# Eight edits to the order of work in a fused recurrence and mixture-of-experts kernel on one core

## The chip, the cores and the metric

The kernel runs on one core of a Trainium2 chip, in one launch. The metric is device time in microseconds (us), the median of repeated executions. A core has TensorE (PE, matmuls and their weight loads, PEld), VectorE (DVE), ScalarE (ACT), GpSimd (POOL) and SyncE (SP), each of which takes its instructions in its own program order, and DMA queues that the engines issue to. Loads go out on SP's queue, some on POOL's and ACT's.

## The reference

```python
# 1. recurrence, B=4, H=8, S=768, D=40 (fp32)
for t in range(S):
    y[:, :, t] = einsum('bhd,bhde->bhe', r_t, state)
    Sa = einsum('bhde,bhe->bhd', state, a_t)
    state = state * w_t[:, :, None, :] - einsum('bhd,bhe->bhde', Sa, b_t) + einsum('bhd,bhe->bhde', v_t, k_t)
x = y.transpose(0, 2, 1, 3).reshape(3072, 320)
# 2. first MoE: 320 -> 1536 -> 320
x = ((x @ w_a) * (x @ w_b)) @ w_out
# 3. second MoE: 8 experts, the best one for each token
logits = x @ w_gate;  expert_idx = argmax(logits);  g = softmax(logits)[expert_idx]
out = g * (maximum(x @ w1[expert_idx], 0) @ w2[expert_idx])     # 320 -> 1024 -> 320
```

## The kernel before

The 768 steps of the recurrence are done in 12 chunks of 64. Each matmul on fp32 data is made of three or more matmuls on split values: a high part, and the rest that the high part leaves.

`phase1` walks through 13 rounds `c` of 24 slots `i`. In round `c` it runs the main stages of chunk `c` for the four batches in two pairs, prepares chunk `c+1` (the inverse of a 64x64 triangular matrix: DVE steps `tmp`, `xt`, lines 716 and 722, between transposes `t`, line 755, and matmuls `ta`, line 759), `c+2` and `c+3` (loads, range checks, cumulative decays), and lays the matmuls of MoE 1's up-projection (`pm`, line 1115, two groups of eight in each odd slot) between them. Slots of the tables `STEADY`, `LAST` (round 12) and `FIRST` (round 0) say when a piece is issued. The order on PE, DVE, ACT and POOL is the order in which the code issues it; `dv.later(n, f)` and `ot.later(n, f)` put a piece off by `n` slots. SP's order is left to a scheduler that follows the data.

What the change touches:

- **xf.** `stage5` transposes a pair's result into `pz` (PSUM, pool psA of five buffers). DVE multiplies it by the decays into `xf` (line 957) `dxf` slots later. Three slots after stage5, ACT copies `xf` to `xh` (line 1093) and POOL makes `xl` (line 1094), the inputs of `pm`. The next stage0 transposes `sgp_u` (line 666) into the buffer that `pz` gives back, and so waits for `xf`.
- **Range checks.** `spans` (line 557) is four ACT instructions `junk<-w` for each chunk, which wait for the load of `w` (line 534, SP, slot 7). ACT also copies `pm` out as `ua` (line 1118).
- **Output weights' conversion.** `wout` is a list of steps, 60 of them, on 15 pieces: a load `rawo` of 256 KB (line 1060, SP), DVE `c_f` (line 429) and ACT `c_k` (line 431), and more on DVE and ACT. `T["wout"][i]` says how many are taken in slot `i`: seven in a round, from chunk 2 on, in slots 1, 2, 6, 17, 19, 20, 22 and 23. The finished weights (`wo`, DRAM) are read by `load_w` (line 1160, POOL's queue).
- **Gates (round 12).** `gate_steps` makes eight more columns of the output weights: DVE adds the two parts to `gf` (line 1204), PE transposes it (`gt`, line 1217), ACT copies (`gft`, line 1219), PE multiplies by the gate's weights (`pg`, line 1233), ACT copies (`gs`, 1236), PE transposes (`pg`, 1225), and ACT `wh` and DVE `wl` (lines 1239 and 1240) write the columns, which the first products `py` (line 1268) read.
- **MoE 1, down.** `load` brings a tile `hf` of the hidden layer, 512 KB (line 1247, SP, three buffers); `conv` makes `hh` on ACT and `hl` on DVE (lines 1257, 1258), and then calls `load(i + 3)`. Each tile feeds 24 products `py`, and three tiles make a unit of 256 tokens. After a unit DVE chooses the expert and computes the token's place (lines 1281 to 1316), and POOL scatters the rows (line 1321).
- **MoE 2's first weights.** Towards the end of MoE 1 `first` issues the loads `r1` (lines 1452 to 1454) and `r2` (line 1460) of expert 0's weights and gathers the first rows (`x_head`, line 1515); ACT and POOL split them (lines 1469 to 1475, 1483, 1484).

Of the kernel before, what the change touches and what calls it, by code (L numbers as in the profile page):

```python
# [31 lines left out]
FIRSTX = [5, 7, 3, 8, 10]  # L32
# [7 lines left out]
def kernel_body(tc, I, out, stage="full", dbg=None):  # L40
    nc = tc.nc
    ctx = ExitStack()
    with ctx:
# [36 lines left out]
        with ExitStack() as moe:  # L80
            with tc.manual_schedule(engines={E.PE, E.DVE, E.Activation, E.Pool}):
                down = None if stage == "up" else MoeDown(tc, I, moe, psA, psM, ident, hT, wo, xs)
                phase1(tc, I, cst, drm, psA, psM, ident, hT, mk_ident, wo, xs, span, tiny, down)
                if stage == "up":
                    return
                experts = Experts(tc, I, moe, psA, psM, ident, xs, out)
                down.run(experts, span, tiny, flag)
# [45 lines left out]
def phase1(tc, I, cst, drm, psA, psM, ident, hT, mk_ident, wo, xs, span, tiny, down):  # L133
# [7 lines left out]
    def run(fs):  # L141
        for f in fs:
            f()

    conv = M.weight_steps()
    wout = M.wout_steps(wo)
# [68 lines left out]
    for c in range(NCH + 1):  # L215
        T = dict(STEADY)
# [9 lines left out]
        for i in range(24):  # L226
            run(ot.take())
            if c == NCH and down:
                if i == LAST["free"]:
                    mid.close()  # L230
                    down.begin()
                    M.spare = down.p2
                if i >= LAST["gate"]:
                    run(down.gate_steps(1))
                for j in range(3):
                    if i == LAST["load"][j]:
                        down.load(j)
                for j in range(2):
                    if i == LAST["w"][j]:
                        down.load_w(4 * j + 4)  # L240
                    if i == LAST["conv"][j]:
                        down.conv(j)
# [16 lines left out]
            if c < NCH and i == T["uload"][1]:  # L259
                A.uload(c, 1)  # L260
            if c == NCH - 1 and i == LAST["open"] and down:
                att.close()
# [79 lines left out]
            more = []  # L342
            if c < 2:
                more = conv.take(T["conv"][i] if c == 0 else FIRST["conv1"][i])
            elif c < NCH:
                more = wout.take(T["wout"][i])
            if 2 <= c < 10 and i == T["fill"] - 2:
                A.zero([zt])
            if 2 <= c < 10 and i == T["fill"]:
# [34 lines left out]
    "r0": [19, 21, 23], "r1": [7, 14, 15], "load_r": [10, 1], "score": [7, 8, 15, 19], "row": [11, 21], "relayout": 5,  # L384
    "load_w": 7, "span": [10, 11, 13, 15], "scan": [16, 17, 20, 20, 22], "inverse": 22, "vload": [9, 20], "uload": [19, 7],

    "t21a": [22, 26], "t21b": [24, 28],
    "tinv": [0, 0, 2, 3, 5, 5, 2, 2, 5, 5, 5, 5, 5, 5, 5, 5, 3, 0, 0, 0, 0, 0, 0, 0],
    "group": 2, "fill": 5, "dsg": 2, "dxf": 1, "dtake": 3, "dh": 1, "dst": 3,
}  # L390
LAST = {"open": 21, "free": 6, "w": [1, 17], "load": [14, 16, 19], "gate": 18, "conv": [21, 22]}

FIRST = {
    "order": [
# [740 lines left out]
class MoeDown:  # L1135
# [126 lines left out]
    def product(self, py, i, j, cols):  # L1262

        first, G = i * self.G % self.K, self.G
        s = slice(128 * j, 128 * j + 128)
        for k in range(G):
            for n, (l, r) in enumerate(((1, 1), (0, 0), (1, 0))):
                self.nc.tensor.matmul(  # L1268
                    py, self.pair[i][l][:, k, s], self.W[r][:, first + k, cols],
                    start=(first + k == 0 and n == 0), stop=(first + k == self.K - 1 and n == 2))  # L1270
# [149 lines left out]
class Experts:  # L1420
# [64 lines left out]

    def first(self, i):

        ops = [(i + 2, lambda: self.load1(0)), (i + 2, lambda: self.load2(0)), (i + FIRSTX[0], lambda: self.head(0)),
               (i + FIRSTX[1], lambda: self.head(1)), (i + FIRSTX[4], lambda: self.head(2))]
        ops += [(i + FIRSTX[2] + k, lambda k=k: self.split1(0, k)) for k in range(3)]  # L1490
        ops += [(i + FIRSTX[3] + k, lambda k=k: self.split2(0, k)) for k in range(4)]
        return ops
# [407 lines left out]
```

## Time and profile before

| | |
|---|---|
| median of 3 runs | 1096.92 us (1094.73 to 1098.28) |
| profiled execution | 1096.91 us, of which the span is 1095.2 us and 1.7 us lie around it |
| busy | PE 88%, PEld 84%, DVE 65%, ACT 52%, POOL 36% |
| mean granted TensorE clock | 0.938 of full speed |

One slice of the page's table is 27.4 us. The granted clock of a stretch is given as a share of 2.4 GHz, so 0.50 is 1.2 GHz. In a row of the timeline the brackets hold the engine's idle time before the instruction, and what ended it.

### The profile page before, as it was taken

The page shows a single profiled execution, that of the slowest core. Times are in us where ns is not written, and L with a number is a line of the kernel's source. Part 1 is how long each engine was busy: PE and PEld are TensorE (multiplying, and loading weights), DVE is VectorE, ACT ScalarE, POOL GpSimd, SP SyncE. Part 2 cuts the span into 40 slices and gives each one's busy share as a digit, 9 for nine tenths or more (in the row PEclk, how much of TensorE's full clock was granted, in tenths as well). Part 3 has the DMA queues.
Part 4 walks back from the last instruction along what each step waited for, and adds up shares of the span by engine and source line. Part 5 has one row for each costly group of instructions (what it writes and reads, how often), then busy time and mean ns, then how long its engine had stood idle before and what let it go on. Part 6 is the DMA issues. An engine that isn't in the chain of part 4 may idle for free.

```text
span 1095.2 us, 28147 instructions
## 1 busy us (share of the span) xinstructions
PE 968.2 (88%) x10879; PEld 915.2 (84%) x10879; DVE 713.9 (65%) x1891; ACT 572.7 (52%) x1365; POOL 397.4 (36%) x433
## 2 busy tenths in 40 slices
PE   4045478899999999999999999999998899999994
PEld 4045477799999998999999999899998899999994
DVE  8799689698989878898986832346566642222230
ACT  5357767566666666656665453333334254444540
POOL 4336444324233232324232112002215377666641
PEclk9656579899999999999999999999999999999998
DMA  8563453658696867769584234635566364444500
GB/s 206 154 163 92 101 139 99 162 120 195 139 196 153 189 169 145 183 132 199 133 181 122 64 83 134 204 114 170 179 195 190 112 215 129 147 149 143 159 16 17
DMA packets 218667, 158.59 MB, mean 145 GB/s; under 512 B 125269, under 2 KB 200630, under 8 KB 218524
## 3 DMA queue, kind: packets, MB, share of 16 engines
q1 hardware_dynamic: 205196, 137.33, 49.4%
q0 software_dynamic: 9808, 15.76, 4.7%
q10 hardware_dynamic: 3520, 3.61, 1.2%
q8 instruction: 88, 1.44, 0.6%
q14 instruction: 55, 0.45, 0.2%
HBM read 108.08 MB, written 44.60 MB: 139 GB/s over the span
## 4 chain that ended last, share of the span: by engine, by line
PE 62%; DVE 13%; DMA 8%; issue 6%; ACT 4%; POOL 4%; SPq 1%; POOLq 0%; DVEq 0%; ACTq 0%
PE pm L1115 21%; PE py L1268 10%; PE u L1562 6%; PE dn L1582 5%; PE s1p L631 3%; DVE tmp L716 3%; PE p L907 3%; DVE xt L722 3%; PE pp L891 2%; DMA out<-y,ids 2%; PE py L936 2%; PE px L836 2%; POOL l L1484 1%; PE ta L759 1%; DMA hf<-hT 1%
## 5 line engine op out<-in xcount | busy, mean ns | idle before, releaser
L716 DVE TENSOR_TENSOR tmp<-m,xt 128x126 f32<-128x126 f32 (+22 forms) x372 | 117.2, 315 | 33.1 <-DMA m<-nd 24.7
L1565 DVE SCALAR_TENSOR_TENSOR hl<-u,hh 128x384 fp32r<-128x384 f32 (+5 forms) x72 | 41.5, 580 | 139.7 <-ACT hh L1564 139.7
L1115 PE MATMUL pm<-xl,wh 128*128 128x256 f32 x576 | 130.8, 309 | 1.8 <-ACT ua L1118 1.2
L722 DVE TENSOR_TENSOR xt<-xt,tmp 128x126 f32<-128x126 f32 (+22 forms) x372 | 113.4, 305 | 9.1
L1115 PE MATMUL pm<-xh,wl 128*128 128x256 f32 x576 | 117.5, 286 | 0.0
L1115 PE MATMUL pm<-xh,wh 128*128 128x256 f32 x576 | 116.8, 285 | 0.0
L1127 DVE TENSOR_TENSOR uh<-pm,ua 128x256 f32<-128x256 f32 x144 | 59.6, 415 | 61.5 <-PE pm L1115 42.7
L1115 PEld LDWEIGHTS pm<-xl,wh 128*128 128x128 f32 x576 | 89.3, 193 | 7.6 <-ACT ua L1118 2.1
L1268 PE MATMUL py<-wh,hl 128*128 128x328 f32 x288 | 91.6, 318 | 3.3 <-DVE hl L1258 3.3
L1268 PE MATMUL py<-wl,hh 128*128 128x328 f32 x288 | 92.4, 321 | 0.6 <-DVE wl L1240 0.6
L1268 PE MATMUL py<-wh,hh 128*128 128x328 f32 x288 | 91.6, 318 | 0.0
L1115 PEld LDWEIGHTS pm<-xh,wh 128*128 128x128 f32 x576 | 91.2, 194 | 0.0
L1115 PEld LDWEIGHTS pm<-xh,wl 128*128 128x128 f32 x576 | 91.0, 194 | 0.0
L1115 PE MATMUL pm<-xl,w 128*128 128x256 f32 x288 | 82.5, 286 | 0.0
L1115 PE MATMUL pm<-xh,w 128*128 128x256 f32 x288 | 82.4, 286 | 0.0
L919 POOL TENSOR_SCALAR_AFFINE_SELECT s<-s 64x512 f32<-64x512 f32 x56 | 43.7, 781 | 102.1 <-ACT s L917 99.6
L759 PE MATMUL ta<-t,s 32*32 32x32 f32 x768 | 23.1, 200 | 59.9 <-DVE t L755 56.2
L1321 POOL DMA_INDIRECT xs<-xr,si x24 | 28.3, 1181 | 131.2 <-DVE acc L1316 77.4
L1118 ACT COPY ua<-pm 128x256 f32<-128x256 f32 x144 | 53.6, 372 | 42.6 <-PE pm L1115 39.5
L641 POOL TENSOR_SCALAR_AFFINE_SELECT s<-s 64x512 f32<-64x512 f32 x48 | 33.7, 702 | 115.3 <-ACT s L639 109.5
L1582 PE MATMUL dn<-l,hh 128*128 128x320 f32 (+3 forms) x240 | 75.0, 312 | 0.0
L1582 PE MATMUL dn<-h,hl 128*128 128x320 f32 (+3 forms) x240 | 74.0, 309 | 0.0
(276 smaller groups left out, 2810.7 us busy)
## 6 DMA issues: line engine op xcount, KB each, us to landing
hT<-uh SPq DMA_DIRECT2D x72, 256.0 KB
hf<-hT SPq DMA_DIRECT2D x36, 512.0 KB
r<-in_moe_w SPq DMA_DIRECT2D x8, 1280.0 KB
r<-in_moe_w SPq DMA_DIRECT2D x8, 1024.0 KB
bk<-in_bk SPq DMA_DIRECT2D x22, 360.0 KB
xs<-zt SPq DMA_DIRECT2D x8, 805.0 KB
m<-nd SPq DMA_DIRECT2D x44, 128.0 KB
at<-in_a SPq DMA_DIRECT2D x24, 180.0 KB
```

The source lines that it names most:

```text
L641: nc.gpsimd.affine_select(out=v, in_=v, pattern=[[0, 8], [1, C]], base=0, channel_multiplier=-1, compare_op=ALU.is_gt, fill=0.0)
L716: nc.vector.tensor_tensor(box[0], m[2 * s // R][:, s % (R // 2):s % (R // 2) + 1, s + 1:].to_broadcast([128, rows, n]), xt[:, :rows, s:s + ...
L722: nc.vector.tensor_tensor(xt[:, :rows, s + 1:], xt[:, :rows, s + 1:], box[0], op=ALU.subtract)
L759: nc.tensor.matmul(pa[b % 2][urow(b, R), R * h:R * h + R], s1[b % 2][urow(b, 0), h, R:C], t11[urow(b, 0), h, :], start=True, stop=True)
L919: nc.gpsimd.affine_select(out=s2t[q * C:q * C + C], in_=s2t[q * C:q * C + C], pattern=[[0, 8], [1, C]], base=0, channel_multiplier=-1, com ...
L1115: nc.tensor.matmul(p, l, r, start=(i == 0), stop=(i == len(seq) - 1))
L1118: nc.scalar.copy(a, p)
L1127: nc.vector.tensor_tensor(h[:, f % 2], p, a, op=ALU.mult)
L1268: self.nc.tensor.matmul(py, self.pair[i][l][:, k, s], self.W[r][:, first + k, cols], start=(first + k == 0 and n == 0), stop=(first + k == ...
L1562: nc.tensor.matmul(p, l, r, start=(i == 0), stop=(i == len(seq) - 1))
L1565: nc.vector.scalar_tensor_tensor(out=hl, in0=p, scalar=0.0, in1=hh.bitcast(F32), op0=ALU.max, op1=ALU.subtract)
L1582: nc.tensor.matmul(p, l[:, q], r[:, f], start=(f == 0 and i == 0), stop=(f == len(hs) - 1 and i == 2))
```

## The change

Eight numbers are changed: xf is computed in the slot of its transposes instead of the next; the first of the four range checks goes from slot 10 to 11; chunk 2 takes no step of the output weights' conversion before slot 5, so its first is in slot 6; in round 12 the second load of output weights is called in slot 11 instead of 17, the three first tiles `hf` in 18, 20 and 22 instead of 14, 16 and 19, and the gates start in slot 14 instead of 18; and `r2` is called three products later.

```diff
             elif c < NCH:
-                more = wout.take(T["wout"][i])
+                more = wout.take(T["wout"][i] if c > 2 or i > 4 else 0)
...
-    "load_w": 7, "span": [10, 11, 13, 15], "scan": [16, 17, 20, 20, 22], "inverse": 22, "vload": [9, 20], "uload": [19, 7],
+    "load_w": 7, "span": [11, 12, 13, 15], "scan": [16, 17, 20, 20, 22], "inverse": 22, "vload": [9, 20], "uload": [19, 7],
...
-    "group": 2, "fill": 5, "dsg": 2, "dxf": 1, "dtake": 3, "dh": 1, "dst": 3,
+    "group": 2, "fill": 5, "dsg": 2, "dxf": 0, "dtake": 3, "dh": 1, "dst": 3,
 }
-LAST = {"open": 21, "free": 6, "w": [1, 17], "load": [14, 16, 19], "gate": 18, "conv": [21, 22]}
+LAST = {"open": 21, "free": 6, "w": [1, 11], "load": [18, 20, 22], "gate": 14, "conv": [21, 22]}
...
-        ops = [(i + 2, lambda: self.load1(0)), (i + 2, lambda: self.load2(0)), (i + FIRSTX[0], lambda: self.head(0)),
+        ops = [(i + 2, lambda: self.load1(0)), (i + 5, lambda: self.load2(0)), (i + FIRSTX[0], lambda: self.head(0)),
```

DVE at the start of chunk 2, before (`c_f` is the conversion's first instruction, `t` the transposes for chunk 3's inverse, `bk` the scaling of chunk 4):

```order
L621 TENSOR_TENSOR bk4_0_2121<-bk4_0_2121,suf4_2183 120x6x64
L429 TENSOR_SCALAR c_f_2524<-rawo0_2449 128x256
L755 STREAM_TRANSPOSE t11_2_1_2576<-s1_2_1_1273 32x256 x2
L621 TENSOR_TENSOR bk4_0_2121<-bk4_0_2121,suf4_2183 120x6x64
L716 TENSOR_TENSOR tmp3_0_2601<-m3_2420,xt3_2421 128x31
```

The same place now:

```order
L621 TENSOR_TENSOR bk4_0_2121<-bk4_0_2121,suf4_2183 120x6x64
L755 STREAM_TRANSPOSE t11_2_1_2568<-s1_2_1_1273 32x256 x2
L716 TENSOR_TENSOR tmp3_0_2592<-m3_2422,xt3_2423 128x31
L621 TENSOR_TENSOR bk4_0_2121<-bk4_0_2121,suf4_2183 120x6x64
L722 TENSOR_TENSOR xt3_2423<-xt3_2423,tmp3_0_2592 128x31
```

The instruction `c_f` now comes 28 rows later, behind the first nine steps of chunk 3's inverse.

DVE in round 12, before, from `gf3` on (`uh` is the output of an up-projection, `hl` the low part of a tile `hf`):

```order
L1204 TENSOR_TENSOR gf3_11399<-wh_11026,wl_11027 128x640
L1258 TENSOR_TENSOR hl0_11436<-hf0_11280,hh0_11435 128x1024
L1204 TENSOR_TENSOR gf4_11461<-wh_11026,wl_11027 128x640
L1258 TENSOR_TENSOR hl1_11484<-hf1_11304,hh1_11483 128x1024
L1127 TENSOR_TENSOR uh11_8_11376<-pm11_9_1_11452,ua11_9_11450 128x256
L1204 TENSOR_TENSOR gf5_11490<-wh_11026,wl_11027 128x640
L1127 TENSOR_TENSOR uh11_10_11546<-pm11_10_1_11537,ua11_10_11535 128x256
L1127 TENSOR_TENSOR uh11_10_11546<-pm11_11_1_11560,ua11_11_11556 128x256
L1240 TENSOR_TENSOR wl_11027<-pg_11481,wh_11026 128x12x8
```

The same engine now, from `gf3` on:

```order
L1204 TENSOR_TENSOR gf3_11349<-wh_11026,wl_11027 128x640
L1204 TENSOR_TENSOR gf4_11405<-wh_11026,wl_11027 128x640
L1127 TENSOR_TENSOR uh11_6_11326<-pm11_7_1_11396,ua11_7_11394 128x256
L1204 TENSOR_TENSOR gf5_11430<-wh_11026,wl_11027 128x640
L1127 TENSOR_TENSOR uh11_8_11486<-pm11_8_1_11477,ua11_8_11475 128x256
L1258 TENSOR_TENSOR hl0_11526<-hf0_11427,hh0_11525 128x1024
L1240 TENSOR_TENSOR wl_11027<-pg_11425,wh_11026 128x12x8
L1258 TENSOR_TENSOR hl1_11557<-hf1_11506,hh1_11556 128x1024
L1127 TENSOR_TENSOR uh11_8_11486<-pm11_9_1_11542,ua11_9_11540 128x256
```

All of `gf` now stands ahead of `hl0`, and `wl` ahead of the last three `uh`.

SP's loads towards the end of MoE 1, before (`hf32` to `hf35` are the last tiles):

```order
L1454 DMA r1_0_12822<-in_moe2_w1 64x1024
L1460 ISA
L1460 DMA r2_0_12826<-in_moe2_w2 128x8x320
L1247 DMA hf32_12882<-hT_67 128x4x256
L1247 DMA hf33_12937<-hT_67 128x4x256
L1247 DMA hf34_12969<-hT_67 128x4x256
L1515 ISA
L1515 DMA x_head_12971<-xs_72 128x2x322
L1247 DMA hf35_13032<-hT_67 128x4x256
```

And now:

```order
L1454 DMA r1_0_12822<-in_moe2_w1 64x1024
L1247 DMA hf32_12880<-hT_67 128x4x256
L1247 DMA hf33_12935<-hT_67 128x4x256
L1460 ISA
L1460 DMA r2_0_12969<-in_moe2_w2 128x8x320
L1247 DMA hf34_12967<-hT_67 128x4x256
L1515 ISA
L1515 DMA x_head_12971<-xs_72 128x2x322
L1247 DMA hf35_13032<-hT_67 128x4x256
```

The load `r2` changes places with `hf32` and `hf33`.

## Rows read from the trace of the kernel before

**Rows 1.** The page: busy us; slices in tenths; one group (busy, mean ns | idle).
```profile
PE 968.2 (88%) x10879; PEld 915.2 (84%) x10879; DVE 713.9 (65%) x1891; ACT 572.7 (52%) x1365; POOL 397.4 (36%) x433
...
PE   4045478899999999999999999999998899999994
...
PEclk9656579899999999999999999999999999999998
...
L716 DVE TENSOR_TENSOR tmp<-m,xt 128x126 f32<-128x126 f32 (+22 forms) x372 | 117.2, 315 | 33.1 <-DMA m<-nd 24.7
```
**Rows 2.** Stretches: start:end and length in us, busy us (instructions), PEclk, DMA share, GB/s.
```profile
211.00:214.40 3.40, 3.40 (x20) 3.18 (x20) 1.65 (x9) 1.72 (x4) 0.00 (x0) 0.50 0.45 125
504.00:553.00 49.00, 47.87 (x713) 45.10 (x714) 43.32 (x113) 31.55 (x82) 15.62 (x21) 1.00 0.73 164
695.30:715.35 20.05, 17.21 (x214) 13.91 (x212) 8.50 (x13) 10.21 (x35) 0.00 (x0) 0.91 0.33 103
706.00:709.30 3.30, 3.30 (x22) 3.13 (x15) 1.28 (x3) 1.50 (x6) 0.00 (x0) 0.50 0.75 217
716.20:719.55 3.35, 3.35 (x15) 3.35 (x14) 1.01 (x1) 0.00 (x0) 0.00 (x0) 0.50 0.34 96
842.50:845.85 3.35, 3.35 (x14) 3.35 (x14) 2.67 (x15) 2.12 (x5) 0.86 (x2) 0.50 0.13 49
```
**Rows 3.** What PE waited for: us in total, times, longest.
```profile
PE px L827 <- DVE xf L957: 5.3, 1, 5.3
...
PE sgp_u L666 <- DVE xf L957: 3.1, 6, 1.1
...
PE gt_l L1217 <- DVE gf L1204: 1.4, 1, 1.4
...
PE py L1268 <- DVE wl L1240: 0.6, 1, 0.6
```
**Rows 4.** Timeline of DVE at the start of chunk 2: start, us, instruction [idle before].
```profile
208.86 0.29 DVE L429 TENSOR_SCALAR c_f<-rawo 128x256 int32<-128x256 int32 x1 [6.53 <-DMA rawo<-in_moe_w_out]
```
**Rows 5.** Timeline of PE at the start of chunk 2.
```profile
209.64 0.22 PE L759 MATMUL ta<-t,s 32*32 32x32 f32 x2 [3.29 <-DVE t L755]
```
**Rows 6.** The chain that ended last: start, us, what.
```profile
202.72 6.12 DMA rawo<-in_moe_w_out
...
210.76 3.48 PE pm L1115 x16
...
216.72 2.11 PE pm L1115 x16
...
417.75 7.97 DMA w<-in_w
...
819.85 12.92 DMA hf<-hT
```
**Rows 7.** Timeline of PE in chunk 6.
```profile
425.94 0.26 PE L666 MATMUL sgp_u<-ident,sgT 56*120 56x56 f32 x1 [1.08 <-DVE xf L957]
...
428.58 0.50 PE L1115 MATMUL pm<-xl,wh 128*128 128x256 f32 x2 [0.94 <-ACT ua L1118]
```
**Rows 8.** Timeline of ACT in chunk 6.
```profile
425.75 0.62 ACT L557 ACTIVATE junk<-w,wlim 120x384 bf16<-120x384 f32 x1 [3.72 <-DMA w<-in_w]
```
**Rows 9.** Timeline of DVE in round 12.
```profile
702.63 1.23 DVE L1258 TENSOR_TENSOR hl<-hf,hh 128x1024 fp32r<-128x1024 f32 x1 [3.19 <-ACT hh L1257]
```
**Rows 10.** Timeline of POOL in round 12.
```profile
682.43 0.76 POOL L1160 DMA_DIRECT2D wl<-wo  x1
```
**Rows 11.** DMA issues from 640 to 720 us: count, KB each, median us to landing.
```profile
wl<-wo POOLq DMA_DIRECT2D x3, 640.0 KB, 9.4
```
**Rows 12.** Timeline of PE near the end of MoE 1.
```profile
841.78 0.42 PE L1268 MATMUL py<-wh,hl 128*128 128x328 f32 x1 [2.42 <-DVE hl L1258]
```
**Rows 13.** Timeline of DVE near the end of MoE 1.
```profile
835.27 2.18 DVE L1310 TENSOR_TENSOR t<-t,base 128x16 f32<-128x16 f32 x1
```
**Rows 14.** Timeline of POOL near the end of MoE 1.
```profile
834.65 2.77 POOL L1471 TENSOR_TENSOR l<-r,h 128x1024 fp32r<-128x1024 f32 x1
```

## The prediction

> **What bounds the kernel now.** First the page's slices [rows 1]. PE is half idle up to about slice 8, that is up to 210 us at 27.4 us a slice; from there it stands at 9 almost to the end. So after 210 us an edit is worth what it takes from PE's waits, or gives back of PE's clock. Then the stretches [rows 2]. In a piece of a steady chunk (504 to 553 us) PE is busy 47.87 of 49.00 us at clock 1.00: all that waits cost there is 1.1 us in 49, so edits to steady chunks can't win much. Four stretches of 3.4 us have the granted clock at 0.50: the 211.0, the 706.0, the 716.2 and the 842.5 us one. PE is busy all through them, so they are found by the clock and not by idle time. Before each of them PE had just waited: 3.29 us [rows 5], 1.37 of the total at the gates' `gt` [rows 3], 0.62 at the `py` after the gates' `wl` [rows 3], and 2.42 us [rows 12]. Sixteen `pm` that took 2.11 us at full clock took 3.48 us in the first [rows 6]; at half clock a stretch of 3.4 us does the work of 1.7 us, so each costs up to 1.7 us. Waits of 1.08 and 0.94 us in chunk 6 [rows 7] were followed by no such stretch, so a short wait doesn't always bring it. Last, the list of waits [rows 3] and the chain [rows 6] say what ended each wait.
>
> **The change, part by part.** The sum is made against the profiled execution, 1096.91 us, which is the median of the runs shown (1096.92).
>
> *Conversion from slot 6 in chunk 2.* The load `rawo` takes 6.12 us [rows 6] and DVE sits idle 6.53 us in front of the conversion's first `c_f`, until 208.86 [rows 4]. Behind it on DVE stands `t`, and PE waits 3.29 us for that `t` [rows 5]; the low clock follows [rows 2]. Now `t` stands ahead of `c_f`, with 28 rows between the old place and the new. Nineteen of them are `tmp` and `xt` at about 315 ns [rows 1], some 6 us, so the load has landed when `c_f` comes. Removed: 3.29 + 1.7 = 5.0 us. It is less if `t` or what follows it waits for another load of the same moment; then 2 us. Not more than 5.5, with the gain of the ACT work that stood behind `c_k`. The conversion is two steps late from here to its end in chunk 9, and `wo` is read only in chunk 11, so that costs nothing. I take 5.0.
>
> *xf a slot sooner, first range check a slot later.* `sgp_u` waits for `xf` 3.1 us in six places [rows 3], all in the steady chunks. Now `xf` stands ahead of two or three `tmp` and `xt` of DVE, 0.6 to 0.9 us by the mean of 315 ns of a `tmp` [rows 1]. That is more than five of the six waits, which share 3.1 − 1.1 = 2.0 us, and less than the sixth, 1.08 us [rows 7]. In chunk 6 PE also waits 0.94 us for a `ua`, because ACT sat 3.72 us before a range check [rows 8] whose `w` took 7.97 us [rows 6]. With the check a slot later the copies `kb` and `ua` come ahead of it. But the conversion's shifted place also moves one `rawo` of 256 KB on SP ahead of `uv` and `w`: at the 164 GB/s of the steady stretch [rows 2] it is 1.6 us that `w` may come later, about what a slot gives. So I count chunk 6's 2.02 us as 1.3 us left, and the rest of the 3.1 us (2.0) as gone: 0.7 + 1.9 = 2.6 us. Bounds 0 (all of it goes to `w`) and 3. In chunk 0 an early `xf` could shorten `px`'s wait of 5.3 us [rows 3]; but PE is half idle there and DVE sets the pace, so I take 0, with 1 us to either side.
>
> The Trainium skill (DMA: Bandwidth & Descriptors, "Queues, rings and completion order") says that on each engine the descriptors of one queue are taken in the ring's order; by it the moved `rawo` does delay `w`, and the estimate of 1.6 us would be in full; no row here shows a `w` right behind a `rawo`.
>
> *Gates.* From 695.30 to 715.35 us PE is busy 17.21 of 20.05 us [rows 2]: waits of 2.84 us, 1.4 of them for `gf` and 0.6 for `wl` [rows 3]. Here `gf4` stands on DVE behind `hl0`, which itself waits 3.19 us for ACT's `hh` [rows 9]. Now all `gf` stand ahead of `hl0`, and three groups `pm` cover the last chain from `pg` over `gs` to `wl`. The adds `gf` come about four slots sooner and need their weights: the last part is issued at 682.43 [rows 10] and lands 9.4 us later [rows 11], near 692, or some microseconds after that. `gf4` stood behind `hl0` at 702.63 + 1.23 = 703.9; four slots, that is two lots of 16 `pm` at 2.11 us [rows 6], sooner it is wanted near 699.6, which leaves about 7 us. `hf2` reuses the buffer of `hf0` and now waits for `conv(0)`, but PE wants it only after two tiles of 24 products each. Of the 2.84 us I leave 0.8 for the step from the last `pm` to `py`, and both low stretches go: 2.0 + 1.7 + 1.7 = 5.4 us. From below: if the weights come late or a wait of a microsecond stays and the clock falls, 0. From above: 2.84 + 3.4 = 6.2.
>
> *Order of loads at the end of MoE 1.* `hf32` was issued right behind `r2` and takes 12.92 us [rows 6]. So `hl32` came late, and the chain that chooses the place of the tokens ran into POOL's subtractions: `t` took 2.18 us from 835.27 on while POOL's `l` ran from 834.65 for 2.77 us [rows 13, 14]; a second `t` fared alike. Behind them stands `hl33`, for which PE waits 2.42 us [rows 12], and then the clock falls [rows 2]. Now `hf32` and `hf33` go ahead of `r2`. Ahead of it or with it were `r1` and `r2`, 1536 and 1280 KB by their shapes, beside its own 512: by bytes `r2`'s share of the 12.92 us is 1280/3328, that is 5.0 us. So `hf32` lands near 828 instead of 832.8. The chain `t` is then over at about 834, before POOL's `l`, and `hl33` stands when PE wants it, at 841.78 − 2.42 = 839.4. `hf34` behind `r2` lands when it did before. Gain 2.42 + 1.7, less 0.4 for a new short wait for `x_head` or `hf34`: 3.7 us. Bounds: −1 (`hf34` waits for `r2` in full, and the clock falls for longer) and 5.
>
> The Trainium skill (SBUF — State Buffer, "Who interferes with whom") says that a DVE instruction with two inputs in SBUF contends with a GpSimd instruction that reads SBUF, and that the one that issues first keeps the shared ports till it ends. Rows 13 and 14 agree: `t` ended 0.03 us after `l`. By it the gain holds only while the chain `t` is wholly ahead of `l`; if the two shift together, 3.7 becomes 0.
>
> **Sum.** 5.0 + 2.6 + 5.4 + 3.7 = 16.7 us; 1096.9 − 16.7 = 1080.2. The forecast is 1080 us; its own range is 1076 to 1085.
>
> **Rivals.**
>
> 1. *The clock falls all the same.* The low stretches come after any wait in these four places, and a wait of half a microsecond stays in each. For: the 0.62 us before `py` was enough. Against: 1.08 and 0.94 us in chunk 6 were not [rows 7]. Then 4 × 1.7 = 6.8 us of the sum go: 1087.
> 2. *The stall moves.* `hf2` lands late behind `conv(0)` when other loads run (12.92 us is possible [rows 6]), or POOL's subtractions move with the chain `t`, and `hf34` waits for `r2`. For: rows 13 and 14, where DVE pays for POOL. Against: POOL waits for `r1`, which isn't moved. Then one or both of the last two parts are lost: 1080.2 + 5.4 = 1085.6, or + 3.7 more = 1089.
> 3. *Slower: the range checks wait for a `w` that comes behind `rawo`.* In chunk 6 an ACT wait of 3.72 us [rows 8] cost PE 1.08 + 0.94 = 2.02 us [rows 7]. The same in each of six chunks (3 to 8), with `w` later by the 6.12 us that a `rawo` takes [rows 6], would cost up to 4.5 us a chunk more, 27 us: 1080.2 + 27 = 1107. It decides from (1096.9 − 1080.2) / 6 = 2.8 us a chunk on. Against: the rest of the steady stretch leaves ACT a third idle [rows 2], and the check itself is a slot later.
> 4. *The edits do nothing that shows.* Each of the four waits is replaced by another of its length; the time stays at about 1096.
>
> **Chances.** Forecast 0.60, rival 1 0.16, rival 2 0.12, rival 3 0.07, rival 4 0.05. The range is 1074 to 1090: below it reaches to all upper bounds of the parts but 1 us each (5.5 + 3 + 6.2 + 5 = 19.7, and chance of a gain in chunk 0), above it takes in rivals 1 and 2. About 0.3%, 3.3 us, is what a measurement can tell from no change. Faster than 1093.6: 0.88; within 1093.6 to 1100.2: 0.05; slower: 0.07.
>
> **What would show it.** The clock at 1.00 throughout the former four stretches; `ta` at the start of chunk 2 without its 3.29 us and `c_f` without its 6.53; `sgp_u` waiting for `xf` under 1.5 us in all; no wait over 0.7 us between the last `pm` of round 12 and the first `py`; `hf32` landing near 828 us and `hl33` without a wait behind it. The prediction is wrong if the waits of `junk` for `w` grow by more than 2 us each and PE waits with them; if a low-clock stretch stays at the gates; or if PE waits more than 2 us in chunks 9 to 11 or for `hf2`, `hf34` or `x_head`.

## The result

The changed kernel takes 1086.37 us, the median of 7 runs (1080.34 to 1090.43), against 1096.92 us (1094.1 to 1101.27, 7 runs): ratio 0.9898, 95% interval 0.9869 to 0.9928. That is 10.5 us, with the interval 8 to 14 us; the forecast was 16.9 us, to 1080 us. The measured time lies inside the stated range of 1074 to 1090 us, but outside the forecast's own range of 1076 to 1085, and by its number alone it could as well be rival 1 (1087) or rival 2 (1085.6). The runs of one kernel differ by 10 us, and this turned out to be the main lesson.

The page of the profiled execution (1086.37 us), busy time and slices of 27.1 us, answers to [rows 1]:

```profile
span 1084.6 us, 28183 instructions
...
PE 961.4 (89%) x10879; PEld 909.3 (84%) x10879; DVE 705.0 (65%) x1891; ACT 572.8 (53%) x1365; POOL 391.6 (36%) x433
...
PE   4145389899999999999999999999999999999994
...
PEclk9655669999999999999999999999999999999998
```

The same matmuls keep PE busy 6.8 us less. The four stretches at low clock (0.50, that is 1.2 GHz) that before had between 210 and 850 us are gone. Stretches (columns as in [rows 2]): the start of chunk 2, one in chunk 5, a steady piece, the gates from the first `gt` to the first `py`, one in MoE 2:

```profile
202.00:210.00 8.00, 7.66 (x154) 7.03 (x151) 3.34 (x14) 6.14 (x16) 2.08 (x3) 1.00 0.92 261
374.50:377.70 3.20, 3.20 (x30) 2.81 (x32) 2.96 (x10) 2.83 (x9) 1.00 (x1) 0.53 0.74 204
504.00:553.00 49.00, 48.21 (x711) 45.37 (x709) 42.88 (x121) 31.16 (x80) 14.52 (x20) 1.00 0.76 170
687.31:707.44 20.13, 19.67 (x244) 16.61 (x244) 9.00 (x14) 10.46 (x37) 0.00 (x0) 1.00 0.40 117
848.90:852.20 3.30, 3.30 (x18) 3.30 (x18) 0.99 (x3) 0.77 (x2) 0.97 (x1) 0.54 0.10 37
```

Two low stretches are new, at 374.5 and 848.9 us. Two fewer of 3.4 us give back up to 3.4 us of the 6.8; the rest isn't traced to a place. What PE waits for now:

```profile
PE pm L1115 <- ACT ua L1118: 3.6, 4, 2.1
...
PE pb L1607 <- DVE hl L1565: 1.8, 1, 1.8
PE pr L1303 <- DVE hl L1565: 1.4, 1, 1.4
...
PE sgp_u L666 <- DVE xf L957: 1.0, 1, 1.0
```

`sgp_u` went from 3.1 us to 1.0, a single wait at 171.8 us, ahead of the steady chunks, and `gt` and `py` behind `wl` are off the list [rows 3], but `pm` waits 3.6 us for `ua` (1.2 before).

To see where the gain arises, the span is cut at instructions that both kernels have: the first transpose `pz` of chunk 2, the second pair's of chunk 9, the product `py` number 216 of MoE 1 (each matmul `py` counts as one, from 0 on), its number 648, and the `u` of MoE 2 with the numbers 0 and 144. Lengths in us, each between two starts in one trace; the 66.13 us from product 216 to product 648 are equal in all traces. In the last column is the time at low clock in the four parts of the kernel: chunk 2's start, the steady chunks, the gates, the loads and MoE 2 to `u` 144. The experiments below are in the same table. Each row is one execution and not always a typical one: "changed, again" is the longest of its six runs, "conversion in step" the shortest of its six, "r2 alone" the shortest of its twelve, and "conversion alone" the longest of its eleven (1116.57 us, the next is 1107.64), which the ratio of that kernel leaves out.

| kernel (edits) | to chunk 2 | chunks 2 to 9 | to product 216 | 648 to first u | to u 144 | low clock |
|---|---|---|---|---|---|---|
| before | 227.9 | 364.0 | 158.0 | 39.3 | 46.5 | 3.4, 0, 6.8, 3.4 |
| changed | 222.8 | 364.8 | 152.7 | 35.8 | 49.3 | 0, 3.4, 0, 3.4 |
| changed, again | 224.4 | 362.0 | 152.6 | 40.0 | 51.6 | 0, 3.4, 0, 6.8 |
| conversion in step | 222.5 | 358.9 | 152.7 | 35.7 | 48.4 | 0, 0, 0, 3.4 |
| all but the conversion | 230.1 | 359.5 | 152.7 | 35.8 | 46.7 | 6.8, 0, 0, 0 |
| conversion alone | 223.9 | 391.1 | 156.6 | 37.5 | 46.2 | 0, 41.0, 3.4, 0 |
| all but range checks | 222.6 | 365.1 | 152.7 | 40.3 | 48.6 | 0, 3.4, 0, 3.4 |
| all but xf | 222.4 | 360.4 | 152.7 | 41.7 | 48.0 | 0, 0, 0, 6.8 |
| round 12 alone | 226.3 | 361.7 | 152.6 | 39.5 | 48.1 | 3.4, 0, 0, 3.4 |
| r2 alone | 225.6 | 362.1 | 155.0 | 36.8 | 46.1 | 6.8, 0, 0, 0 |
| split of r1 later alone | 229.2 | 366.2 | 155.0 | 40.9 | 49.0 | 6.8, 3.4, 0, 6.8 |
| in step, split later | 222.6 | 359.0 | 152.7 | 40.4 | 48.3 | 0, 0, 0, 6.8 |
| the same, verdict sooner | 223.4 | 361.0 | 152.6 | 38.5 | 48.1 | 0, 0, 0, 3.4 |
| in step, no xf | 224.0 | 360.4 | 152.7 | 40.0 | 48.7 | 0, 0, 0, 3.4 |

Between the two first traces the parts stand at −5.1, +0.9, −5.3, −3.6 and +2.8 us. With −0.3 in what follows `u` 144 that is −10.6 us of span.

### The profile page after: what moved, and what is told of

The parts are those of the page before. It is cut to its first block, busy times and chain, and to the rows that moved or that the text cites. A ratio compares the mean times of both kernels' runs of the same rounds, so it can differ in the third digit from the quotient of the medians.

```text
span 1084.6 us, 28183 instructions
## 1 busy us (share of the span) xinstructions
PE 961.4 (89%) x10879; PEld 909.3 (84%) x10879; DVE 705.0 (65%) x1891; ACT 572.8 (53%) x1365; POOL 391.6 (36%) x433
## 3 DMA queue, kind: packets, MB, share of 16 engines
q8 instruction: 88, 1.44, 0.6%
## 5 line engine op out<-in xcount | busy, mean ns | idle before, releaser
L919 POOL TENSOR_SCALAR_AFFINE_SELECT s<-s 64x512 f32<-64x512 f32 x56 | 43.6, 778 | 117.7 <-ACT s L917 115.3
L1582 PE MATMUL dn<-h,hh 128*128 128x320 f32 (+3 forms) x240 | 74.1, 309 | 0.0
## 6 DMA issues: line engine op xcount, KB each, us to landing
xs<-zt SPq DMA_DIRECT2D x8, 805.0 KB, 10.4
```

What stands on the lines that cost most here:

```text
L919: nc.gpsimd.affine_select(out=s2t[q * C:q * C + C], in_=s2t[q * C:q * C + C], pattern=[[0, 8], [1, C]], base=0, channel_multiplier=-1, com ...
L1582: nc.tensor.matmul(p, l[:, q], r[:, f], start=(f == 0 and i == 0), stop=(f == len(hs) - 1 and i == 2))
```

## The experiments

Each was timed beside the kernel before on the same chip; the ratio is to that.

**The changed kernel again.**

> The changed kernel once more, with all eight edits. It shows how far the parts of the gain repeat. If they are the kernel's own, the places stand to the kernel before as in the first profile: -5.1 us at the transposes pz of chunk 2, -4.2 at those of chunk 11, -9.5 at the 216th product py, -13.1 at the first u of MoE 2, -10.3 at the end of PE. If the loss of 3 us in chunk 5 or the loss of 2.8 us after the first u is chance, one of the two will be absent or in another place.

1084.28 us (1080.17 to 1092.47, 6 runs), ratio 0.9887 (0.9849 to 0.9925). Chunk 2 (no low clock, 1.6 us longer) and the gates (0.1 us) repeat. The stretch from product 648 to `u` doesn't (40.0 us, 4.2 more than in the first trace), and steady chunks and MoE 2 differ by 3 and 2 us. So the parts from 648 on can't be read from one trace.

**The conversion back in step.**

> All eight edits, but the conversion makes up its two lost steps in slots 9 and 11 of chunk 2, so that from chunk 3 on its loads rawo stand on SP where they stood before the change, not ahead of uv and w. Theory 1 (the steady chunks lost because a rawo now stands ahead of w): -5.1 us at chunk 2, then the gain grows to -7 or -8 at chunk 11, no wait of a range check for w over 4 us, and the time comes near 1083 us. Rival (the earlier xf and the later range check lost it themselves): as in the changed kernel, -4.2 us at chunk 11 and about 1086 us.

```diff
-                more = wout.take(T["wout"][i] if c > 2 or i > 4 else 0)
+                more = wout.take((T["wout"][i] if c > 2 or i > 4 else 0) + (c == 2 and i in (9, 11)))
```

1081.77 us (1079.54 to 1088.45, 6 runs), ratio 0.9877 (0.9839 to 0.9914). Chunks 2 to 9 take 358.9 us, 5.1 less than in the first trace of before and 3 to 6 less than in the two traces of the changed kernel. By chunk 11 the gain is 10.4 us, more than the 7 or 8 of theory 1, and no range check waits over 1.5 us for `w`. So the trace bears theory 1 out; the times don't tell this kernel from the changed one (0.9877 against 0.9887, intervals that overlap). The total of ACT's waits of the range checks for `w`, from the view of the tile `junk`, in this kernel and in the changed one:

```profile
  DMA w<-in_w: 4.2, 6
```
```profile
  DMA w<-in_w: 15.0, 7
```

One pair of traces wouldn't be enough for this: with the old order of loads and the old check, the total is 10.8, 4.5, 5.4 and 13.2 us in four traces. But with the later check it is 4.2 to 4.7 us in all five traces that have `rawo` in its old place, and 15.0, 12.6 and 8.3 us in the three that have it ahead of `w`.

**All but the conversion's edit, and that edit alone.**

> All edits but that of the conversion, which starts in slot 1 of chunk 2 as before. Theory 1: no gain at chunk 2 (the wait of 3.3 us and the low clock are back), -2 to -3 us at chunk 11, and about 1088 us. Rival: no gain at chunk 2, +0.9 us at chunk 11, about 1091.5 us.

1085.64 us (1084.32 to 1086.51, 6 runs), ratio 0.9896 (0.9865 to 0.9928). Chunks 2 to 9 take 359.5 us, as with the conversion in step, and `ta` at chunk 2 waits 3.08 us for `t` again. At chunk 11 the gain is 2.2 us, as theory 1 has it.

> The kernel before with the conversion's later start alone. Both theories: -5.1 us at chunk 2. Theory 1: range checks wait longer for w than the 10.8 us in all of before, and 1 to 4 us of the gain are lost again by chunk 11, so 1093 to 1096 us. Rival: -5.1 us all the way, about 1092 us.

1105.80 us (1096.12 to 1116.57, 11 runs), ratio 1.0064 (1.0038 to 1.0090): slower than before. Both theories were too mild. By the ratio the loss is 7 us net (4 to 10), that is about 12 us beside a gain of 4.6 at chunk 2. Its one trace is of the 1116.57 us, so it shows the mechanism, but not its usual size: chunk 2 comes after 223.9 us, 4.0 sooner than in before, and chunks 2 to 9 take 391.1 us, 27 more than before. The other ten runs had a mean granted clock of 0.934 (0.929 to 0.941), the sixteen of before beside them 0.938 (0.933 to 0.944), so some low clock belongs to the usual run too. SP, then ACT and PE, in chunk 5 of this kernel:

```profile
372.57 0.60 SPq L1060 DMA_DIRECT2D rawo<-in_moe_w_out  x1
373.27 1.73 SPq L798 DMA_DIRECT2D uv<-in_vt  x2
375.18 0.44 SPq L534 DMA_DIRECT2D w<-in_w  x1
```
```profile
383.81 0.62 ACT L557 ACTIVATE junk<-w,wlim 120x384 bf16<-120x384 f32 x1 [3.78 <-DMA w<-in_w]
```
```profile
384.30 0.26 PE L666 MATMUL sgp_u<-ident,sgT 56*120 56x56 f32 x1 [1.44 <-DVE xf L957]
...
386.64 0.58 PE L1115 MATMUL pm<-xl,wh 128*128 128x256 f32 x1 [0.65 <-ACT ua L1118]
```

`rawo` goes out right before `uv` and `w`, the check waits for `w`, and PE waits twice within 3 us. From the issue of `w` to the start of the check that waits for it, it takes 8.6 us here (375.18 to 383.81) and 8.7 on the mean of the seven chunks that wait (8.2 to 9.1); in before it takes 7.2 on the mean of six (6.6 to 8.0). The clock is low for 10 us in each of three chunks:

```profile
331.80:341.90 10.10, 9.67 (x104) 9.20 (x105) 5.55 (x20) 7.16 (x20) 1.66 (x2) 0.51 0.47 138
386.40:396.50 10.10, 9.86 (x105) 9.39 (x105) 5.66 (x21) 6.97 (x18) 1.66 (x2) 0.51 0.52 147
441.10:451.20 10.10, 9.51 (x103) 9.04 (x104) 5.55 (x20) 7.17 (x20) 1.61 (x2) 0.51 0.53 143
```

With the shorter ones it is 41 us at half clock, up to 20 us of work lost. From chunk 2 to 9 PE is idle 17.2 us, 10.3 more than in before, and busy 16.7 us longer for the same matmuls: these are the 27 us. This is rival 3 of the prediction, at under half its price by the ratio (12 of 27 us), in a kernel that has only one of the edits. The edit moves the conversion's steps on DVE and ACT as well as its loads, and no run moves the loads alone; that the loads do the harm rests on the checks' waits for `w`.

**Which steady edit holds it back.**

> All edits but that of the range checks: the first stays in slot 10. The conversion's later start alone lost 27 us from chunk 2 to chunk 9 while its loads rawo stood ahead of w, and with all edits the same stretch lost 0.9 and gained 1.9 us in two looks; so one of the other two steady edits holds the loss back. Theory 1 (the later range check does, since ACT then copies kb and ua before it waits for w): a loss of over 10 us from chunk 2 to 9, with sgp_u waiting for xf, and a time over 1095 us. Rival (the earlier xf does, since sgp_u then no longer waits behind ACT and DVE): a loss under 4 us there, and 1084 to 1089 us.

1087.48 us (1081.49 to 1092.37, 12 runs), ratio 0.9954 (0.9932 to 0.9976); chunks 2 to 9: 365.1 us.

> All edits but that of xf, which stays in the slot after its transposes. Theory 1 (the later range check holds the loss back): 0 to 3 us lost from chunk 2 to chunk 9, about 1085 to 1089 us. Rival (the earlier xf does): over 10 us lost there, over 1095 us.

1082.31 us (1079.10 to 1086.60, 6 runs), ratio 0.9912 (0.9885 to 0.9939); chunks 2 to 9: 360.4 us.

Neither theory stands as it was put: in neither trace do ten microseconds go, so either edit is enough to hold most of the loss back. By the times the later check matters more: the two kernels, timed beside each other, are 5.2 us apart by their medians, with intervals that just overlap. Whether the kernel without the later check gives up half of the gain of all edits (0.9954 against 0.9887 and 0.9898) is less sure: the kernel with all edits wasn't timed on this chip, where the kernel before takes 1091.19 us instead of 1097.42.

What PE waits for changes with the edits. In these two traces the earlier `xf` without the later check leaves it waiting for `ua` (4.2 us in all), the later check without the earlier `xf` for `uh` (3.9 us), and `sgp_u` doesn't wait for `xf` at all there, though `xf` stands in its old slot. With both missing, in the kernel above, PE waits for `xf` 9.3 us and for `ua` 5.7 us.

**Round 12 alone, r2 alone.**

> The kernel before with the edits of round 12 alone (gates, weights, first tiles). Theory: nothing up to chunk 11, then -5.3 us at the 216th product py, of which 2 are waits and 3.4 two stretches of low clock, and about 1092 us. Rival (the gates gain only where the work before them comes sooner): under 3 us of gain, and a wait for gf or for a tile hf.

1088.47 us (1084.26 to 1090.16, 12 runs), ratio 0.9973 (0.9958 to 0.9989). To product 216 it takes 152.6 us, as all kernels with this edit do (152.6 to 152.7). But the four traces of kernels without it have 158.0, 156.6, 155.0 and 155.0. The waits were the same 1.37 and 0.62 us in all four; the low clock that followed them lasted 6.8, 3.4, 0 and 0 us. The gates' waits in the kernel with r2 alone, and the clock of the stretches behind them:

```profile
700.54 0.27 PE L1217 MATMUL gt_l<-ident,gf 64*128 64x64 f32 x1 [1.37 <-DVE gf L1204]
...
709.77 0.42 PE L1268 MATMUL py<-wl,hh 128*128 128x328 f32 x1 [0.62 <-DVE wl L1240]
```
```profile
700.60:704.00 3.40, 3.40 (x53) 2.91 (x54) 2.29 (x3) 1.68 (x7) 0.00 (x0) 1.00 0.68 192
709.80:713.20 3.40, 3.40 (x23) 3.40 (x24) 1.23 (x1) 0.57 (x1) 0.00 (x0) 1.00 0.11 21
```

So the edit is worth 2.3 us without low clock and up to 5.4 with it, 3.5 on the mean of these four; by the times it is 0.27%, 3 us. The theory's 5.3 us was before's draw, and the rival's wait for `gf` or `hf` isn't there.

> The kernel before with the later load r2 alone. Theory 1: up to the 744th product nothing, then -3.5 to -4.7 us at the 816th, and the wait of 2.4 us for hl gone; about 1093 us. Rival (the stall moves with POOL's subtractions, as one look on the changed kernel shows a wait of 2.3 us for hl again): 0 to -1 us at the 816th product, about 1097 us.

1090.36 us (1086.87 to 1094.40, 12 runs), ratio 0.9994 (0.9976 to 1.0012): no change. In its trace the stretch is 36.8 us, 2.5 less than before: theory 1 by the trace, the rival by the times. The traces together show what goes with the length of the stretch. ACT's first copy from `r1` stands ahead of `hh` and waits for the load. In the three kernels with all of `r2`'s edit that took 35.7 to 35.8 us it came 4.0 to 4.3 us after product 648; in those that took 40.0 to 41.7 us it came 7.1 to 8.8 us after it. ACT in the changed kernel and in the one without the xf edit:

```profile
810.67 1.05 ACT L1469 CAST h<-r 128x1024 fp32r<-128x1024 f32 x1 [1.58 <-DMA r<-in_moe_w]
```
```profile
810.36 1.05 ACT L1469 CAST h<-r 128x1024 fp32r<-128x1024 f32 x1 [6.18 <-DMA r<-in_moe_w]
```

Product 648 starts at 806.40 and 801.56 us in these. Without the edit it is 37.5 us (copy at 4.8) and 39.3 and 39.5 us (7.5 and 7.1). So with `r1` early the later `r2` gains about 1.8 us, and with `r1` late it loses 0.5 to 2.3, by a few traces each.

**The split later.**

> The kernel before with one edit of another kind: ACT's and POOL's split of r1 is put off by one product (24 matmuls), r2 stays where it was. In the traces so far the stretch from the 648th product to the first u took 35.7 to 37.5 us where ACT's first copy from r1 came up to 5.3 us after that product, and 39.3 to 41.7 us where it came after 7 us or more, with the later r2 or without. Theory 1 (ACT waits for r1 and the tiles' copies hh wait behind it): the stretch takes 35.5 to 38 us here though r2 isn't moved, ACT waits under 1 us for r1. Rival (the tiles themselves come late in those runs, with all loads): 39 us or more, with waits of hh for hf.

1098.81 us (1092.94 to 1106.15, 12 runs), ratio 1.0020 (0.9998 to 1.0042). The stretch takes 40.9 us: the theory fails. ACT waits 1.6 us for `r1` instead of 4.9 (under 1 was expected), but POOL's subtractions now lie together, and `hl` runs into them. DVE and POOL:

```profile
834.02 5.32 DVE L1258 TENSOR_TENSOR hl<-hf,hh 128x1024 fp32r<-128x1024 f32 x1 [3.67 <-ACT hh L1257]
```
```profile
833.54 4.70 POOL L1471 TENSOR_TENSOR l<-r,h 128x1024 fp32r<-128x1024 f32 x2
```

PE waits 4.22 us for it. The edit moved two things, so it doesn't tell whether a landing of `r1` in time would be enough.

> All eight edits, the conversion's two steps made up in chunk 2, and the split of r1 one product later. Theory 1: -10 us at chunk 11 against the first profile of before, 35.5 to 36.5 us from the 648th product to the first u, and about 1079 us. Rival: that stretch at 39 us or more, about 1083 us.

1085.14 us (1081.89 to 1087.85, 6 runs), ratio 0.9891 (0.9869 to 0.9913). Chunks 2 to 9 repeat (359.0 us); the stretch is 40.4 us, the rival's number, and the kernel is no better. This time DVE stands idle until `x_head` lands, and the `hl` queued behind it then takes 3.36 instead of 1.22 us beside POOL's subtractions; PE waits 3.49 us for it:

```profile
824.27 0.18 DVE L1523 TENSOR_SCALAR ids<-x_head 128x2 int32<-128x2 f32 x1 [5.49 <-DMA x_head<-xs]
...
824.57 3.36 DVE L1258 TENSOR_TENSOR hl<-hf,hh 128x1024 fp32r<-128x1024 f32 x1
```

**The verdict sooner.** In MoE 2 the verdict on the range checks is formed: DVE writes `bb`, PE multiplies it into `pb`. In the changed kernel DVE's `bb` stood 3.93 us, until the second of POOL's two subtractions ended, and PE waited for the `hl` queued behind it, 1.85 us. DVE, POOL and PE:

```profile
867.89 3.93 DVE L1599 TENSOR_SCALAR bb<-sp 120x4 bf16<-120x4 f32 x1
```
```profile
867.02 4.77 POOL L1471 TENSOR_TENSOR l<-r,h 128x1024 fp32r<-128x1024 f32 x2
```
```profile
872.69 0.17 PE L1607 MATMUL pb<-bb,ones 128*128 128x6 bf16 x1 [1.85 <-DVE hl L1565]
```

> The kernel of the run before with the verdict's instructions on DVE (bb) one matmul group sooner, ahead of POOL's subtractions for expert 1. In two looks of ten at these kernels bb stood 3.9 and 4.8 us behind POOL's l, and PE waited 1.8 and 2.7 us for what stood behind it. Theory 1 (bb loses the shared ports to l): bb under 0.5 us and no wait of PE at pb, about 1 us less on the mean. Rival (bb is slow for another reason): 1.3 us or more again.

```diff
-                put(up, 2, self.late)
+                put(up, 1, self.late)
```

1081.00 us (1079.51 to 1085.39, 5 runs), ratio 0.9856 (0.9837 to 0.9874), the lowest of all; beside it the kernel of the run before stood at 0.9891 (0.9869 to 0.9913). `bb` is now ahead of POOL's `l`, and PE has no wait at `pb`:

```profile
865.74 0.17 DVE L1599 TENSOR_SCALAR bb<-sp 120x4 bf16<-120x4 f32 x1
```
```profile
867.26 4.77 POOL L1471 TENSOR_TENSOR l<-r,h 128x1024 fp32r<-128x1024 f32 x2
```

So theory 1 stands for `bb`. The 4 us between the two medians are more than it can explain, and the intervals overlap: to `u` 144 the two traces differ by 0.2 us (48.3 and 48.1), since in that of the run before `bb` took 1.29 us and PE had no wait at `pb` either.

> All edits with the conversion's two steps made up, but xf in the slot after its transposes as before. With rawo away from w the steady chunks 2 to 9 gained 5.1 us in one look with the earlier xf. Theory 1 (the earlier xf does it): 1 to 2 us gained there, the rest of sgp_u's waits for xf is back. Rival (the later range check does it, as all edits but xf gained 3.6 us there): 3.5 us or more.

1083.96 us (1081.13 to 1086.97, 6 runs), ratio 0.9881 (0.9862 to 0.9900). Chunks 2 to 9: 360.4 us, 3.5 less than before's first trace, on the rival's edge. `sgp_u` doesn't wait for `xf`, against theory 1. With the earlier `xf` it is 358.9, 359.0 and 361.0 us in three traces with the conversion in step, so `xf` is left with 0.8 us on the mean, in a part that differs by 2 to 3 us between traces of one order. With the conversion out of step and `xf` late, above, it was 360.4 us as well: in these two traces the place of `rawo` costs nothing without the earlier `xf`.

## Why the prediction came out as it did

**Conversion from slot 6: right at its place.** Forecast −5.0, measured −5.1 in the first pair of traces, and 4.6 by the means of the kernels without the edit (five traces, 225.6 to 230.1) and with it (nine, 222.4 to 224.4). `ta`'s wait of 3.29 us and the low clock are gone. As the text allowed for, DVE met another load next: the first `tmp` waits for `m`, and PE is still busy 7.66 of the 8.00 us from 202 to 210 (above).

```profile
206.73 0.19 DVE L716 TENSOR_TENSOR tmp<-m,xt 128x31 f32<-128x31 f32 x1 [4.01 <-DMA m<-nd]
```

Between the old and the new place of `c_f` stand 17 `tmp` and `xt`, not 19; it begins at 215.72 us and doesn't wait.

"The conversion is two steps late from here to its end ... so that costs nothing" is a step that failed. Two steps late means that in each chunk a `rawo` goes out ahead of `w`, and alone that costs about 12 us by the ratio. With all edits the conversion's later start brings nothing that the times can tell (0.9896 without it, 0.9887 and 0.9898 with it). By the means of the traces most of the 4.6 us that it wins at chunk 2 is lost in the steady chunks: 3.8 us, from 359.6 with the old order of loads (four traces) to 363.4 (two). In step the kernel stands at 0.9877.

**xf and range check: the waits went, the term missed.** Forecast −2.6 (0 to −3), measured +0.9 and −1.9 in two traces. (By the text's own parts, 0.7 and 2.0, it would be −2.7.) The change moves the first two checks, from slots 10 and 11 to 11 and 12, and not the first alone. The delay of `w` was sized rightly, 1.6 us by the text and 1.5 from 7.2 to 8.7 us above. What failed is the step that the later slot makes up for it. In chunk 5 `w` took longer, and PE waited. ACT and PE of the changed kernel:

```profile
373.27 0.62 ACT L557 ACTIVATE junk<-w,wlim 120x384 bf16<-120x384 f32 x1 [4.29 <-DMA w<-in_w]
```
```profile
374.29 0.58 PE L1115 MATMUL pm<-xl,wh 128*128 128x256 f32 x1 [2.13 <-ACT ua L1118]
```

Then the clock fell (0.53 in the stretch shown above): 2.1 + 1.7 = 3.8 us, against [rows 7]. With the order of `rawo` restored the two edits gain 2.9 to 5.1 us in four traces against before's first trace, and three of the four are above their upper bound of 3; so what they are worth was underrated and what the conversion's shift costs was missed. Part of that is before's own: its first trace has the stall of chunk 6 [rows 7, 8], and in three kernels that are unchanged there chunks 2 to 9 took 361.7, 362.1 and 366.2 us. On the means, 363.5 against 359.6, the two edits gain 3.9 us. The step that gave this to the earlier `xf` doesn't hold alone: in the two kernels with the later check and the old `xf`, `sgp_u` has no wait for `xf` either.

The Trainium skill (DMA: Bandwidth & Descriptors, "Queues, rings and completion order"), cited in the prediction, says that each DMA engine takes the descriptors of one ring in order. The traces agree: `w` right behind `rawo` did come late, by 1.5 us on the mean; but they don't tell the order in the ring from a sharing of the bandwidth. The waits of the checks for `w` sum to 15.0 us in the changed kernel and 4.2 with `rawo` back in its place.

A sign that the prediction named for being wrong was half there: the checks' waits for `w` grew by more than 2 us in two of six chunks, and in one of the two PE waited 2.1 us with it.

**Gates: right in this pair, too large as a standing cost.** Forecast −5.4, measured −5.3; but 3.4 of it is counted for 6.8 us of low clock, which four traces of the old gates show as 6.8, 3.4, 0 and 0 us. That the first trace of before had both stretches was luck for the forecast; the mean of the four gives 3.5 us. The waits are gone wholly: `wl` is ready when `py` comes, so nothing is left of the 0.8 us that the text kept for it.

**Loads of MoE 2: right in this trace, not on the mean.** Forecast −3.7, measured −3.6; in eight traces of kernels with the later `r2` and the old split (35.7 to 41.7 us, mean 38.3) and three without (37.5 to 39.5, mean 38.8) the difference is 0.5 us. The step that `hf32` lands near 828, so that `hl33` stands when PE wants it, seems to need `r1` to land early: ACT's wait for it comes ahead of `hh`, and DVE's chain and `hf33` follow; the split put off showed that ACT's wait isn't the whole of it. The rows behind [rows 12 to 14] come from a trace in which it landed late. What decides when `r1` lands wasn't found; the times of the kernel with this edit alone show no gain. So this term, too, was right by luck of the draw. And the gain came another way than forecast. The chain `t` was to be over before POOL's `l`, and it wasn't. DVE and POOL of the changed kernel:

```profile
821.49 3.11 DVE L1310 TENSOR_TENSOR t<-t,base 128x16 f32<-128x16 f32 x1
```
```profile
822.15 2.40 POOL L1471 TENSOR_TENSOR l<-r,h 128x1024 fp32r<-128x1024 f32 x1
```

The Trainium skill (SBUF — State Buffer, "Who interferes with whom"), cited in the prediction, says that a DVE instruction with two inputs in SBUF contends with a GpSimd instruction that reads SBUF. The trace agrees, as `t` again ends just behind `l`, by 0.05 us, though its record begins 0.66 us before that of `l`. What failed is the conclusion that the gain holds only with the chain ahead of `l`. With `acc`, 2.37 us, the chain lost more time than the two `t` of before (2.18 and 2.23), and yet PE waited 0.38 us for the `hl` behind it instead of 2.42. Counted from product 648 the chain had begun 4.3 us sooner, since `hl32` had.

**What no term held.** 2.8 us were given back in MoE 2: the 1.85 us at `pb`, 0.3 behind it, and part of what a low stretch after a wait of 1.42 us can cost (up to 1.7). In the 14 traces `bb` took 3.9 us or more twice, both in the changed kernel, 0.17 us in the kernel that moved it, and 1.3 us otherwise.

**Sum.** 5.1 + 5.3 + 3.6 are 14.0 us of the 14.1 forecast for these three; the miss (16.7 − 10.6 = 6.1 us) is the steady chunks (3.5) and MoE 2 (2.8), less 0.3 behind `u` 144. Of the rivals, 3 was real but held off by either of the other two steady edits, 1 was real in part (the clock fell at two new places), 2 was right in some executions. The range is wider below than its bounds: 1096.9 − 19.7 − 1 is 1076, not 1074.

What stays open is where the rest of the gain in time comes from. All edits but the conversion's gain 1.04%, round 12 alone 0.27% and `r2` alone 0.06%. If the parts add up, and a ratio holds from one chip to another, 0.7% (8 us) is left for `xf` and the range checks; the traces show 3.9 us of it in chunks 2 to 9. No run has these two edits alone.

## What to carry to other kernels

A stall and a fall of the clock that one profile shows are one draw: see whether a second execution has them before the whole of it goes into a sum. A piece of work that starts later stays later, and where its loads share a queue with loads that matter, the order on that queue changes in every round; count that, and put the work back in step. When several edits are made together, one may pay for the harm of another, so that taking them one by one misleads: the conversion's edit alone made this kernel slower, and with the others it cost nothing that the times can tell.

## What was not expected of the hardware

The same two waits of PE, 1.37 and 0.62 us in the same order of instructions, were followed by 6.8, 3.4, 0 and 0 us of low clock in four kernels. In the one trace of the conversion's edit alone, waits of 1.44 us and 0.65 us in chunk 5 went with 10 us at a granted clock of 0.51. Seven runs of the changed kernel ranged over 10 us (1080.3 to 1090.4). Between its two traces the parts differ by 0.1 to 4.2 us, most in the stretch from product 648 to the first `u`, where loads of megabytes and POOL's subtractions meet.
